# dP as rows of four heads in an attention backward pass, and V five heads ahead

## The chip, the cores and the metric

The kernel runs on one core of a Trainium2 chip. A core has five engines that run side by side: TensorE (PE, matmuls; PEld is its weight load), VectorE (DVE), ScalarE (ACT), GpSimd (POOL) and SyncE (SP, which only issues DMAs). They share an on-chip memory of 128 partitions (SBUF); TensorE writes into PSUM, eight banks of 512 fp32 columns in each partition. Sixteen DMA engines carry data between SBUF and the main memory; a 1 MB transfer is cut into sixteen parts, one for each of them, and has landed when the last part has. SP, ACT and POOL each issue transfers in the order of their own program. The metric is the time of one execution on the device, in microseconds (us).

## The reference

The reference is one decode step of a transformer block and its backward pass. Only the attention part matters here. There are 4 batches and 32 heads, so 128 pairs, called heads below (s = 0 to 127); each has a cache K and V of 4096 rows of 128 bf16 numbers, 1 MB each, and a single query row.

```python
scores = einsum("bhqd,bhkd->bhqk", q, k_cache) * Dh ** -0.5
p = softmax(scores)                                    # one row of 4096 per head
o = einsum("bhqk,bhkd->bhqd", p, v_cache)
h = x + o.reshape(...) @ wo                            # then a gated MLP
out, vjp = jax.vjp(f, x, k_cache, v_cache, wq, wo, w1, w3, w2)
grads = vjp(grad_out)
```

The outputs include the gradients of both caches. For one head, with dO the gradient of its output row, they are

- dV = p (a column of 4096) times dO (a row of 128),
- dP = V dO (4096 numbers), c = the sum of dO times o,
- dS = p (dP - c) scale, and dK = dS (a column) times q (a row).

So each head reads K and V in the forward pass, reads V again in the backward pass, and writes dV and dK: 3 MB a head in the backward pass.

## The kernel before

In the forward pass K and V stream through. The backward pass is one loop over the heads. SBUF holds 23 slots of 1 MB that are given out and given back in order; of these up to seven hold V for the loop, the others take dV and dK (`gv`, `gk`) and, early on, things of the forward pass. Position (p, j) of a head is row 32 p + j of its cache, p the partition, j from 0 to 31.

V has to be turned before dP can be computed, since TensorE sums over partitions: 32 transposes a head, in four groups of eight, each group copied back over V by ACT.

```python
def V_T(s, ps, part=range(SJ // GW)):                  # SJ = 32, GW = 8
    ...
    for g in part:
        pt = ps.tile([P, GW, P], BF16, tag="tps", name="pt_tps")
        for i in range(GW):
            nc.tensor.transpose(pt[:, i, :], v[:, g * GW + i, :], ident_b[:])
        nc.scalar.copy(out=v[:, g * GW:(g + 1) * GW, :], in_=pt[:])
```

`front(s)` turns V and computes dP with the turned V as the stationary operand: 32 weight loads of 128x128, each followed by a matmul with the one column of dO. `grad_K(s)` makes dS on VectorE, and dK by an outer product there; `grad_V(s)` makes dV in the same way from P and dO. Rows of dO and q are replicated over the partitions for four heads at a time (`reps`, two buffers of each).

```python
def outer(dst, col2, row):                             # VectorE, 128x4096 outputs
    nc.vector.tensor_tensor(out=dst..., in0=col2..., in1=row..., op=ALU.mult)

def grad_V(s):
    gv = Slot("gv")
    outer(gv.heads(), P2s.pop(s), reps["rdo", s // REP][:, s % REP, :])
    nc.gpsimd.dma_start(out=rows_of(out_3[b, h]), in_=gv.heads())
    ...

def front(s):
    if s % REP == 0:
        replicate(s)
    if s not in VTs:
        V_T(s, psT)
    VT = VTs[s].heads()
    dP_ps = psD.tile([P, SJ], FP32, name="dP_ps", tag="dP")
    for j in range(SJ):
        nc.tensor.matmul(dP_ps[:, j:j + 1], lhsT=VT[:, j, :], rhs=dOT_bf[:, s:s + 1], start=True, stop=True)
    sl = VTs.pop(s)
    (vring if len(V2s) + len(VTs) + len(vring) < NV2 else free).append(sl.i)   # NV2 = 7
    P_pairs(s + 2)                                     # GpSimd: P of a head, each number twice
    bwd[s] = dP_ps

def grad_K(s):
    dP_ps = bwd.pop(s)
    t = bw3.tile([P, SJ], FP32, tag="dSt", name="dSt")
    nc.vector.tensor_scalar(out=t[:], in0=dP_ps[:], scalar1=c_rep[:, s:s + 1], scalar2=scale, ...)
    dS2 = bw3.tile([P, SJ, 2], BF16, tag="dS2", name="dS2")
    nc.vector.tensor_tensor(out=dS2[:], in0=t..., in1=P_all[:, s]..., op=ALU.mult)
    gk = Slot("gk")
    outer(gk.heads(), dS2, reps["rq", s // REP][:, s % REP, :])
    nc.sync.dma_start(out=rows_of(out_2[b, h]), in_=gk.heads())
    gk.give()
```

The loop runs V one head ahead of dK, and dV one head ahead. ACT issues the loads of V (`prefetch`, `load_V2`). dV of heads 0 and 1 is made before the loop.

```python
front(0)
for s in range(NH):
    prefetch()
    if s + 1 < NH:
        ...                                            # load V of s + 1 if it has no slot yet
        front(s + 1)
        if s > 0:
            grad_V(s + 1)
    grad_K(s)
    if s >= S0:                                        # S0 = 21
        step("s", 1 if s < S0 + 38 else 3)             # side work, see below
    elif s >= O0:                                      # O0 = 2
        step("o")
```

The steps are side work woven in between the heads. First come the rest of dO with the turned pages of wo ("o"). Then come 128 small fp32 matmuls for dq, four pages of wq to be read, turned and multiplied, and the gradients of the weights ("s").

Of the kernel before, what the change touches and what calls it, by code (L numbers as in the profile page):

```python
# [9 lines left out]
FP32 = mybir.dt.float32  # L10
BF16 = mybir.dt.bfloat16
ALU = mybir.AluOpType
# [3 lines left out]
G = 2  # L16
# [8 lines left out]
def kernel(  # L25
# [22 lines left out]
    nc = tc.nc  # L48
    P = nc.NUM_PARTITIONS

    B = A_x.shape[0]
    D = A_x.shape[-1]
    H = A_k_cache.shape[1]
# [3 lines left out]
    NH = B * H  # L57
# [4 lines left out]
    SJ = Sk // P  # L62
    FC = F // P
    GW = 8
# [3 lines left out]
    scale = float(Dh) ** -0.5  # L68
# [28 lines left out]
    const = ctx.enter_context(tc.tile_pool(name="const", bufs=1))  # L97
    pers = ctx.enter_context(tc.tile_pool(name="pers", bufs=1))
    small = ctx.enter_context(tc.tile_pool(name="small", bufs=2))
    slotp = ctx.enter_context(tc.tile_pool(name="slotp", bufs=1))  # L100


    free = deque(range(NSLOT))

    class Slot:
# [52 lines left out]
    ident_f = const.tile([P, P], FP32, name="ident_f")  # L158
# [2 lines left out]
    nc.vector.tensor_copy(out=ident_b[:], in_=ident_f[:])  # L161
    ones_f = const.tile([P, P], FP32, name="ones_f")
    nc.gpsimd.memset(ones_f[:], 1.0)
    sel_f = const.tile([P, H], FP32, name="sel_f")
    nc.vector.tensor_copy(out=sel_f[:], in_=ident_f[:, 0:H])
    for q in range(1, P // H):
        nc.vector.tensor_tensor(out=sel_f[:], in0=sel_f[:], in1=ident_f[:, q * H:(q + 1) * H], op=ALU.add)
    onesw = []
    for i in range(2):
        t = const.tile([P, 64], BF16, name=f"onesw{i}")  # L170
        nc.gpsimd.memset(t[:], 0.0)
        nc.gpsimd.memset(t[:, 32 - i:33 - i], 1.0)
        onesw.append(t)

    def ones_window(col):
# [2 lines left out]

    rowg = const.tile([P, 8], FP32, name="rowg")
    nc.vector.tensor_reduce(out=rowg[:], in_=ident_f.rearrange("p (c g q) -> p g c q", c=4, q=4), axis=AX.XY, op=ALU.add)
    quad = const.tile([P, 4], FP32, name="quad")
    nc.vector.tensor_reduce(out=quad[:], in_=ident_f.rearrange("p (q i) -> p q i", q=4), axis=AX.X, op=ALU.add)
    bsum = const.tile([P, P], FP32, name="bsum")
    nc.vector.tensor_copy(out=bsum.rearrange("p (c g q) -> p c g q", c=4, q=4),
                          in_=rowg[:, None, :, None].to_broadcast([P, 4, 8, 4]))
    maskneg = const.tile([P, G], FP32, name="maskneg")
    nc.vector.tensor_scalar(out=maskneg[:], in0=rowg[:, 0:G], scalar1=-1.0, scalar2=1e30, op0=ALU.add, op1=ALU.mult)
    wmask = const.tile([P, G, 32], BF16, name="wmask")  # L190
    nc.gpsimd.memset(wmask[:], 0.0)
    for g in range(G):
        nc.vector.tensor_copy(out=wmask[:, g, 4 * g:4 * g + 4], in_=quad[:])
    selg = const.tile([G, P], FP32, name="selg")

    rstd_x = pers.tile([B, 1], FP32, name="rstd_x")
    xhatT = pers.tile([P, DC, B], BF16, name="xhatT")
    qT_bf = pers.tile([P, NH], BF16, name="qT_bf")
    qrep = pers.tile([P, 4, NH], BF16, name="qrep")
# [4 lines left out]
    P_all = pers.tile([P, NH, SJ], BF16, name="P_all")  # L204
# [53 lines left out]
    with ExitStack() as c0:  # L258
# [38 lines left out]
    psT = c1b.enter_context(tc.tile_pool(name="psT", bufs=2, space=bass.MemoryType.PSUM))  # L297
# [5 lines left out]
    def zq_window(z, m):  # L303
        a = 66 * (m % 2) + 32 + (m % 2) - m
        return z[:, a:a + 32]
# [371 lines left out]
    psT = c1b.enter_context(tc.tile_pool(name="psTm", bufs=4, space=bass.MemoryType.PSUM))  # L677
# [26 lines left out]
    assert not pending  # L704
    c1b.close()
    c1.close()


    pers2 = ctx.enter_context(tc.tile_pool(name="pers2", bufs=1, reuse_waits="tile"))
    O_sb = pers2.tile([NH, Dh], BF16, name="O_sb")  # L710
    dOT_bf = pers2.tile([P, NH], BF16, name="dOT_bf")
# [36 lines left out]
    REP = B  # L748
# [16 lines left out]
    def outer(dst, col2, row):  # L765
        nc.vector.tensor_tensor(  # L766
            out=dst.rearrange("p j (r t) -> p j r t", t=2),
            in0=col2[:, :, None, :].to_broadcast([P, SJ, Dh // 2, 2]),
            in1=row.rearrange("p (r t) -> p r t", t=2)[:, None, :, :].to_broadcast([P, SJ, Dh // 2, 2]),
            op=ALU.mult,  # L770
        )

    def grad_V(s):
        b, h = bh_of(s)
# [3 lines that stand above are left out]
        if s > 1:  # L778
            gv.give()
        else:  # L780
            first_gv.append(gv)
# [140 lines left out]

    with ExitStack() as c2:
        psT = c2.enter_context(tc.tile_pool(name="psT2", bufs=2, space=bass.MemoryType.PSUM))
        psD = c2.enter_context(tc.tile_pool(name="psD", bufs=2, space=bass.MemoryType.PSUM))
        psrep = c2.enter_context(tc.tile_pool(name="psrep", bufs=1, space=bass.MemoryType.PSUM))
        psg = c2.enter_context(tc.tile_pool(name="psg", bufs=2, space=bass.MemoryType.PSUM))
        psx = c2.enter_context(tc.tile_pool(name="psx", bufs=1, space=bass.MemoryType.PSUM))
# [202 lines left out]

        bwd = {}


        def P_pairs(s):
            if s < NH and s not in P2s:
                P2s[s] = bw3.tile([P, SJ, 2], BF16, tag="P2", name="P2")
                nc.gpsimd.tensor_copy(out=P2s[s][:], in_=P_all[:, s, :, None].to_broadcast([P, SJ, 2]))  # L1138

        def front(s):  # L1140
            if s % REP == 0:
                replicate(s)
            if s not in VTs:
                V_T(s, psT)
            VT = VTs[s].heads()
            dP_ps = psD.tile([P, SJ], FP32, name="dP_ps", tag="dP")
            for j in range(SJ):
                nc.tensor.matmul(dP_ps[:, j:j + 1], lhsT=VT[:, j, :], rhs=dOT_bf[:, s:s + 1], start=True, stop=True)  # L1148
            sl = VTs.pop(s)
            (vring if len(V2s) + len(VTs) + len(vring) < NV2 else free).append(sl.i)  # L1150
            P_pairs(s + 2)
            bwd[s] = dP_ps

        def grad_K(s):
            b, h = bh_of(s)
            dP_ps = bwd.pop(s)
            t = bw3.tile([P, SJ], FP32, tag="dSt", name="dSt")
            nc.vector.tensor_scalar(out=t[:], in0=dP_ps[:], scalar1=c_rep[:, s:s + 1], scalar2=scale,  # L1158
                                    op0=ALU.subtract, op1=ALU.mult)
            dS2 = bw3.tile([P, SJ, 2], BF16, tag="dS2", name="dS2")  # L1160
            nc.vector.tensor_tensor(out=dS2[:], in0=t[:, :, None].to_broadcast([P, SJ, 2]),  # L1161
                                    in1=P_all[:, s, :, None].to_broadcast([P, SJ, 2]), op=ALU.mult)
            gk = Slot("gk")
            outer(gk.heads(), dS2, reps["rq", s // REP][:, s % REP, :])
            nc.sync.dma_start(out=rows_of(out_2[b, h]), in_=gk.heads())
            gk.give()

        def prefetch():
            while nv["next"] < NH and vring:
                load_V2(nc.scalar)  # L1170


        O0, S0 = 2, 21
        front(0)
        for s in range(NH):
            prefetch()
            if s + 1 < NH:
                if s + 1 not in V2s and s + 1 not in VTs:
                    load_V2(nc.scalar)
                if s == 0:  # L1180

                    first_gv[0].give()
                front(s + 1)
                if s > 0:
                    grad_V(s + 1)
            grad_K(s)
            if s == 0:
                first_gv[1].give()
            if s >= S0:
                step("s", 1 if s < S0 + 38 else 3)  # L1190
            elif s >= O0:
                step("o")
# [31 lines left out]
```

## Time and profile before

| | |
|---|---|
| time, median of 3 runs | 1721.15 us (1721.13 to 1724.16) |
| span in the profile | 1720.0 us |
| moved by the DMAs | 707.86 MB, mean 412 GB/s |
| busy: PE, DVE, ACT, POOL | 1331.8, 1253.1, 960.3, 414.4 us |
| forward pass, backward pass | up to about 690 us, from about 705 us |

The profile page gives the busy time of each engine, then the span in 40 slices (43 us each) with the busy share in tenths, the TensorE clock that was granted, and the DMA rate; then the chain of work that ended last, and groups of instructions by line. A group's line ends with its busy time, the mean of one instruction in ns, and the idle time of the engine just before it with what released it. Views by stage give the same for any stretch of the span. In the timeline, every line is one instruction or a run of like ones: start, duration, engine, line of the kernel, operation, output and input.

### The profile page before, as it was taken

To read this page: it belongs to the slowest core of one execution; us is meant where nothing else is said; L and a number is where in the kernel's file an instruction comes from. 1 tells how busy PE (TensorE), PEld (TensorE's weight loads), DVE (VectorE), ACT (ScalarE), POOL (GpSimd) and SP (SyncE) were. 2 spreads that over 40 slices of the span, in tenths; PEclk is the share of its full clock that TensorE was granted. 3 is DMA by queue.
4 is the path that set the end of the run, shared out by engine and by line. 5 is a ranking of instruction groups with operands and counts; after the bars stand their busy time and mean duration, and the time that the engine had idled before them with its cause. 6 is when DMAs were issued, how large, how long until landed. Compare 5 with 4: busy or idle time off the path is not lost. (4 is left out here: it accounts for less than half of the span.)

```text
span 1720.0 us, 44172 instructions
## 1 busy us (share of the span) xinstructions
PE 1331.8 (77%) x19124; PEld 1131.8 (66%) x19124; DVE 1253.1 (73%) x1389; ACT 960.3 (56%) x1470; POOL 414.4 (24%) x689
## 2 busy tenths in 40 slices
PE   5889888888888888888788787883677778677852
PEld 4767766766667666877677777773565566555652
DVE  5989899899998997667676776763567557456575
ACT  3455444444454444677655555553676667676752
POOL 1211222222222231231322222321223122212220
PEclk8999999999999999666655555555875565565556
DMA  9999999999999999999999999999999999999996
GB/s 397 418 419 419 419 418 420 418 419 418 412 418 405 418 402 395 380 424 424 424 424 425 424 425 425 424 425 398 411 388 410 422 421 417 404 420 419 419 421 273
DMA packets 101762, 707.86 MB, mean 412 GB/s; under 512 B 11052, under 2 KB 15288, under 8 KB 17600
## 3 DMA queue, kind: packets, MB, share of 16 engines
q1 hardware_dynamic: 63568, 432.04, 60.9%
q0 software_dynamic: 20864, 148.22, 20.6%
q10 hardware_dynamic: 17136, 124.79, 17.7%
q8 instruction: 150, 2.46, 0.5%
q14 instruction: 44, 0.36, 0.1%
HBM read 422.59 MB, written 282.34 MB: 410 GB/s over the span
## 5 line engine op out<-in xcount | busy, mean ns | idle before, releaser
L761 ACT COPY V<-pt_tps 128x1024 bf16<-128x1024 bf16 x512 | 492.5, 1016 | 200.4 <-PE pt_tps L760 175.2
L760 PE MATMUL pt_tps<-ident_b,V 128*128 128x128 bf16 x4096 | 454.1, 293 | 82.9 <-ACT V L761 78.6
L760 PEld LDWEIGHTS <-V 128*128 128x128 bf16 x4096 | 402.7, 138 | 146.2 <-issue 137.1
L766 DVE TENSOR_TENSOR gv<-P,reps 128x4096 bf16<-128x4096 bf16 x125 | 287.2, 2297 | 195.8 <-ACT reps L1129 92.4
L766 DVE TENSOR_TENSOR gk<-dS,reps 128x4096 bf16<-128x4096 bf16 x128 | 294.0, 2297 | 113.5 <-DMA out_dram<-gv 90.8
L433 PE MATMUL M_ps<-PK,Vn 128*128 128x130 bf16 x4096 | 287.4, 223 | 46.4 <-DMA Vn<-in_A_v_cache_dram 44.3
L418 DVE TENSOR_TENSOR PK<-Kn,PK 128x4096 bf16<-128x4096 bf16 x128 | 292.3, 2284 | 31.7 <-POOL PK L414 31.4
L433 PEld LDWEIGHTS <-Vn 128*128 128x128 bf16 x4096 | 254.9, 100 | 67.1 <-DMA Vn<-in_A_v_cache_dram 59.2
L325 DVE STREAM_TRANSPOSE KT<-Kn 128x512 f32<-128x512 f32 (+1 forms) x321 | 250.6, 797 | 0.3 <-issue 0.2
L320 ACT COPY KT<-pt_tps 128x1024 bf16<-128x1024 bf16 x128 | 129.5, 1012 | 192.9 <-PE pt_tps L319 145.7
L777 POOL DMA_DIRECT2D out_dram<-gv x128 | 68.4, 534 | 673.2 <-DVE dSt L1158 581.9
L1148 PE MATMUL dP_ps<-dOT_bf,V 128*128 128x1 bf16 x4096 | 149.9, 166 | 83.4 <-ACT V L761 58.7
L1148 PEld LDWEIGHTS <-V 128*128 128x128 bf16 x4096 | 140.1, 103 | 96.8 <-ACT V L761 70.2
L1138 POOL COPY P<-P_all 128x64 bf16<-128x64 bf16 x125 | 157.8, 1263 | 0.0
L331 POOL TENSOR_TENSOR W<-qrep,wmask 128x128 bf16<-128x128 bf16 x128 | 123.6, 966 | 82.7 <-PE S_ps L351 67.8
L414 POOL COPY PK<-P_all 128x64 bf16<-128x64 bf16 x128 | 32.6, 255 | 421.4 <-ACT P_all L408 418.4
L408 ACT COPY P_all<-pt_P 32x64 bf16<-32x64 bf16 x256 | 52.1, 203 | 58.9 <-PE pt_P L404 56.7
L1129 ACT CAST reps<-rep_ps 128x512 bf16<-128x512 f32 x62 | 36.4, 587 | 83.8 <-PE rep_ps L1126 46.5
L319 PE MATMUL pt_tps<-ident_b,Kn 128*128 128x128 bf16 x1024 | 81.2, 224 | 0.0
L319 PEld LDWEIGHTS <-Kn 128*128 128x128 bf16 x1024 | 62.6, 100 | 25.8 <-issue 25.8
L443 PE MATMUL kP_ps<-PK,onesw 128*32 128x512 bf16 x1024 | 79.4, 387 | 0.0
L351 PE MATMUL S_ps<-KT,W 128*32 128x256 bf16 x1536 | 75.2, 285 | 0.5 <-DVE KT L325 0.2
(239 smaller groups left out, 1284.9 us busy)
## 6 DMA issues: line engine op xcount, KB each, us to landing
Kn<-in_A_k_cache_dram SPq DMA_DIRECT2D x128, 1024.0 KB, 15.7
Vn<-in_A_v_cache_dram SPq DMA_DIRECT2D x128, 1024.0 KB, 16.1
out_dram<-gv POOLq DMA_DIRECT2D x128, 1024.0 KB, 29.0
out_dram<-gk SPq DMA_DIRECT2D x128, 1024.0 KB, 22.7
V<-in_A_v_cache_dram ACTq DMA_DIRECT2D x119, 1024.0 KB, 15.1
V<-in_A_v_cache_dram SPq DMA_DIRECT2D x9, 1024.0 KB, 18.7
wq<-in_A_wq_dram SPq DMA_DIRECT2D x8, 1024.0 KB, 19.0
out_dram<-gw POOLq DMA_DIRECT2D x6, 896.0 KB, 38.3
```

The source lines that it names most:

```text
L319: nc.tensor.transpose(pt[:, i, :], Kn[:, c * GW + i, :], ident_b[:])
L320: nc.scalar.copy(out=KT[:, c * GW:(c + 1) * GW, :], in_=pt[:])
L325: nc.vector.transpose(out=KT[:, c * w_:(c + n) * w_], in_=Kn[:, c * w_:(c + n) * w_])
L331: nc.gpsimd.tensor_tensor(out=W[:, hl], in0=qrep[:, :, s:s + 1].to_broadcast([P, 4, 32]), in1=wmask[:, hl, None, :].to_broadcast([P, 4, 32 ...
L418: nc.vector.tensor_tensor(out=PK[:, :, 0:Dh].rearrange("p j (r t) -> p j r t", t=2), in0=Ks[s].heads().rearrange("p j (r t) -> p j r t", t=2),
L433: nc.tensor.matmul(hold["M"][:], lhsT=Vn[:, j, :], rhs=PK[:, j, :], start=(j == 0), stop=(j == SJ - 1))
L443: nc.tensor.matmul(hold["kP"][32 * q:32 * (q + 1), :, :], lhsT=ones_window(w), rhs=PK[:, j0:j0 + 4, 0:Dh], start=(w == 0 and c == 0), stop ...
L760: nc.tensor.transpose(pt[:, i, :], v[:, g * GW + i, :], ident_b[:])
L761: nc.scalar.copy(out=v[:, g * GW:(g + 1) * GW, :], in_=pt[:])
L766: nc.vector.tensor_tensor(out=dst.rearrange("p j (r t) -> p j r t", t=2), in0=col2[:, :, None, :].to_broadcast([P, SJ, Dh // 2, 2]), in1=r ...
L1138: nc.gpsimd.tensor_copy(out=P2s[s][:], in_=P_all[:, s, :, None].to_broadcast([P, SJ, 2]))
L1148: nc.tensor.matmul(dP_ps[:, j:j + 1], lhsT=VT[:, j, :], rhs=dOT_bf[:, s:s + 1], start=True, stop=True)
```

## The change

dO becomes the stationary operand and the turned V the moving one. A stationary operand of 32 columns, all zero but for one that holds dO, lets a matmul put its result into one row of 32 and add zero to the others; `zq_window(z, m)` is the slice of a zeroed tile that has dO in column m. Four such matmuls sit in the four column groups of the array (`tile_position`). In this way four heads, with two rows for each quarter of their positions, fill rows of one PSUM bank. ACT copies the bank out, four fp32 transposes turn it, and VectorE makes dS of four heads at once. So dK of a group of four can only begin when V of all four heads is through. The loop therefore runs V five heads ahead of dK, and dV three, and replicates rows four heads ahead. It is meant to take 32 weight loads a head away from TensorE and to let VectorE work on when TensorE is held up. Constants of the forward pass move to a pool (`fcon`) that is closed before the backward pass, which makes room.

```diff
-        psD = c2.enter_context(tc.tile_pool(name="psD", bufs=2, space=bass.MemoryType.PSUM))
+        psD = c2.enter_context(tc.tile_pool(name="psD", bufs=1, space=bass.MemoryType.PSUM))
...
+        zd = [bw3.tile([P, 132], BF16, name=f"zd{i}", tag=f"zd{i}", bufs=1) for i in range(B)]
+        for i in range(B):
+            nc.gpsimd.memset(zd[i][:], 0.0)
+        def dO_window(s):
+            nc.gpsimd.tensor_copy(out=zd[s % B][:, 32:132:67], in_=dOT_bf[:, s:s + 1].to_broadcast([P, 2]))
...
+        def rows_out():
+            if "ps" in rows:
+                rows["sb"] = bw3.tile([P, 512], FP32, tag="dPr", name="dPr", bufs=1)
+                nc.scalar.copy(out=rows["sb"][:], in_=rows.pop("ps")[:])
+        def rows_T():
+            if "sb" in rows:
+                sb = rows["t"] = rows.pop("sb")
+                rows["T"] = psD.tile([P, B, P], FP32, tag="dPT", name="dPT_ps")
+                for jj in range(4):
+                    nc.tensor.transpose(rows["T"][:, jj, :], sb[:, jj * P:(jj + 1) * P], ident_f[:])
         def front(s):
-            if s % REP == 0:
-                replicate(s)
+            hl = s % B
             if s not in VTs:
-                V_T(s, psT)
+                for g in range(SJ // GW):
+                    V_T(s, psT, range(g, g + 1))
+                    if hl == 0 and g == 0:
+                        rows_out()
+                    if hl == 0 and g == 2:
+                        rows_T()
             VT = VTs[s].heads()
-            dP_ps = psD.tile([P, SJ], FP32, name="dP_ps", tag="dP")
-            for j in range(SJ):
-                nc.tensor.matmul(dP_ps[:, j:j + 1], lhsT=VT[:, j, :], rhs=dOT_bf[:, s:s + 1], start=True, stop=True)
+            if hl == 0:
+                rows["acc"] = psD.tile([P, 512], FP32, tag="dP", name="dP_ps")
+            dO_window(s)
+            for u in range(2):
+                for c in range(4):
+                    j0 = 8 * c + 4 * u
+                    nc.tensor.matmul(rows["acc"][32 * c:32 * (c + 1), :], lhsT=zq_window(zd[hl], 2 * hl + u),
+                                     rhs=VT[:, j0:j0 + 4, :], start=(hl == 0 and u == 0),
+                                     stop=(hl == B - 1 and u == 1), tile_position=(0, 32 * c))
...
+        def group_dS(g):
+            ...
+            for hl in range(B):
+                nc.vector.tensor_scalar(out=t5[:, hl], in0=T[:, :, 2 * hl:2 * hl + 2, :], scalar1=c_rep[...], scalar2=scale, ...)
+            dS2s[g] = bw3.tile([P, B, SJ, 2], BF16, tag="dS2", name="dS2", bufs=1)
+            nc.vector.tensor_tensor(out=dS2s[g][:], in0=t..., in1=P_all[:, i0:i0 + B]..., op=ALU.mult)
...
-        O0, S0 = 2, 21
-        front(0)
+        O0, S0, L, LV = 2, 21, 5, 3
+        for s in range(L):
+            load_ahead(s)
+            P_pairs(s)
+            front(s)
+            if s < 2:
+                first_gv[s].give()
+            elif s < LV + 1:
+                grad_V(s)
+        group_dS(0)
         for s in range(NH):
...
+            load_ahead(s + L)
+            if s % REP == 0 and s + REP < NH:
+                replicate(s + REP)
+            P_pairs(s + L)
+            if s + L < NH:
+                front(s + L)
+            elif s + L == NH:
+                rows_out()
+                rows_T()
+            if s > 0 and s + LV < NH:
+                grad_V(s + LV)
             grad_K(s)
-            if s == 0:
-                first_gv[1].give()
+            if s % B == B - 1 and s + 1 < NH:
+                group_dS((s + 1) // B)
```

More of the change, by code (lines that the diff above doesn't have):

```diff
@@ L100 @@
     slotp = ctx.enter_context(tc.tile_pool(name="slotp", bufs=1))
+    cF = ExitStack()
+    fcon = cF.enter_context(tc.tile_pool(name="fcon", bufs=1))
     free = deque(range(NSLOT))
@@ L163 @@
     nc.gpsimd.memset(ones_f[:], 1.0)
-    sel_f = const.tile([P, H], FP32, name="sel_f")
+    sel_f = fcon.tile([P, H], FP32, name="sel_f")
     nc.vector.tensor_copy(out=sel_f[:], in_=ident_f[:, 0:H])
@@ L169 @@
     for i in range(2):
-        t = const.tile([P, 64], BF16, name=f"onesw{i}")
+        t = fcon.tile([P, 64], BF16, name=f"onesw{i}")
         nc.gpsimd.memset(t[:], 0.0)
@@ L177, in ones_window @@
         return onesw[i][:, 32 - i - col:64 - i - col]
-    rowg = const.tile([P, 8], FP32, name="rowg")
+    rowg = fcon.tile([P, 8], FP32, name="rowg")
     nc.vector.tensor_reduce(out=rowg[:], in_=ident_f.rearrange("p (c g q) -> p g c q", c=4, q=4), axis=AX.XY, op=ALU.add)
-    quad = const.tile([P, 4], FP32, name="quad")
+    quad = fcon.tile([P, 4], FP32, name="quad")
     nc.vector.tensor_reduce(out=quad[:], in_=ident_f.rearrange("p (q i) -> p q i", q=4), axis=AX.X, op=ALU.add)
-    bsum = const.tile([P, P], FP32, name="bsum")
+    bsum = fcon.tile([P, P], FP32, name="bsum")
     nc.vector.tensor_copy(out=bsum.rearrange("p (c g q) -> p c g q", c=4, q=4),
                           in_=rowg[:, None, :, None].to_broadcast([P, 4, 8, 4]))
-    maskneg = const.tile([P, G], FP32, name="maskneg")
+    maskneg = fcon.tile([P, G], FP32, name="maskneg")
     nc.vector.tensor_scalar(out=maskneg[:], in0=rowg[:, 0:G], scalar1=-1.0, scalar2=1e30, op0=ALU.add, op1=ALU.mult)
-    wmask = const.tile([P, G, 32], BF16, name="wmask")
+    wmask = fcon.tile([P, G, 32], BF16, name="wmask")
     nc.gpsimd.memset(wmask[:], 0.0)
@@ L193 @@
         nc.vector.tensor_copy(out=wmask[:, g, 4 * g:4 * g + 4], in_=quad[:])
-    selg = const.tile([G, P], FP32, name="selg")
+    selg = fcon.tile([G, P], FP32, name="selg")
     rstd_x = pers.tile([B, 1], FP32, name="rstd_x")
@@ L198 @@
     qT_bf = pers.tile([P, NH], BF16, name="qT_bf")
-    qrep = pers.tile([P, 4, NH], BF16, name="qrep")
+    qrep = fcon.tile([P, 4, NH], BF16, name="qrep")
     d_hhT = pers.tile([P, FC, B], FP32, name="d_hhT")
@@ L706 @@
     c1.close()
+    cF.close()
     pers2 = ctx.enter_context(tc.tile_pool(name="pers2", bufs=1, reuse_waits="tile"))
@@ L1130, in replicate @@
                 reps[nm_, i0 // REP] = rt
-        bwd = {}
+        rows = {}
+        dS2s = {}
+        zd = [bw3.tile([P, 132], BF16, name=f"zd{i}", tag=f"zd{i}", bufs=1) for i in range(B)]
[3 more added lines that the diff above has]
+            nc.gpsimd.tensor_copy(out=zd[s % B][:, 32:132:67], in_=dOT_bf[:, s:s + 1].to_broadcast([P, 2]))
         def P_pairs(s):
@@ L1149, in front @@
+            if hl == B - 1:
+                rows["ps"] = rows.pop("acc")
             sl = VTs.pop(s)
             (vring if len(V2s) + len(VTs) + len(vring) < NV2 else free).append(sl.i)
-            P_pairs(s + 2)
-            bwd[s] = dP_ps
+        def group_dS(g):
+            i0 = g * B
+            T = rows.pop("T").rearrange("p jj (c m) -> p c m jj", c=4)
+            t = rows.pop("t")[:, 0:B * SJ].rearrange("p (b j) -> p b j", b=B)
+            t5 = t.rearrange("p b (c u jj) -> p b c u jj", c=4, u=2)
+            for hl in range(B):
+                nc.vector.tensor_scalar(out=t5[:, hl], in0=T[:, :, 2 * hl:2 * hl + 2, :], scalar1=c_rep[:, i0 + hl:i0 + hl + 1],
+                                        scalar2=scale, op0=ALU.subtract, op1=ALU.mult)
+            dS2s[g] = bw3.tile([P, B, SJ, 2], BF16, tag="dS2", name="dS2", bufs=1)
+            nc.vector.tensor_tensor(out=dS2s[g][:], in0=t[:, :, :, None].to_broadcast([P, B, SJ, 2]),
+                                    in1=P_all[:, i0:i0 + B, :, None].to_broadcast([P, B, SJ, 2]), op=ALU.mult)
@@ L1154, in grad_K @@
         def grad_K(s):
             b, h = bh_of(s)
[L1156 to L1162, printed above, removed]
@@ L1163, in grad_K @@
             gk = Slot("gk")
-            outer(gk.heads(), dS2, reps["rq", s // REP][:, s % REP, :])
+            outer(gk.heads(), dS2s[s // B][:, s % B], reps["rq", s // REP][:, s % REP, :])
             nc.sync.dma_start(out=rows_of(out_2[b, h]), in_=gk.heads())
@@ L1170, in prefetch, with load_ahead @@
                 load_V2(nc.scalar)
-        O0, S0 = 2, 21
-        front(0)
-        for s in range(NH):
[L1176 to L1179, printed above, removed]
-                if s == 0:
[L1182 to L1185, printed above, removed]
+        O0, S0, L, LV = 2, 21, 5, 3
+        def load_ahead(s):
+            prefetch()
+            if s < NH and s not in V2s and s not in VTs:
+                load_V2(nc.scalar)
+        for s in range(L):
[7 more added lines that the diff above has]
+        group_dS(0)
+        for s in range(NH):
+            load_ahead(s + L)
[9 more added lines that the diff above has]
+                grad_V(s + LV)
             grad_K(s)
-            if s == 0:
-                first_gv[1].give()
+            if s % B == B - 1 and s + 1 < NH:
+                group_dS((s + 1) // B)
             if s >= S0:
```

## The prediction

> **What bounds the kernel now.** I read the page's 40 slices first, then the busy time by stage, then how DMAs land, then the timeline at the start of the backward pass.
>
> The slices show a kernel that lives on its DMAs:
>
> ```profile
> PEclk8999999999999999666655555555875565565556
> DMA  9999999999999999999999999999999999999996
> GB/s 397 418 419 419 419 418 420 418 419 418 412 418 405 418 402 395 380 424 424 424 424 425 424 425 425 424 425 398 411 388 410 422 421 417 404 420 419 419 421 273
> ```
>
> DMA is full in every slice but the last, at 418 to 425 GB/s; no compute engine is. Clear dips are in slices 13 to 17 (down to 380), 28 to 31 (down to 388) and the last. By stage of the backward pass (start, end, busy us of each engine, clock, DMA share, GB/s):
>
> ```profile
> 688.00:731.00 43.00, 37.66 (x662) 35.20 (x660) 26.63 (x43) 28.81 (x35) 9.80 (x13) 0.68 0.96 380
> 731.00:860.00 129.00, 102.93 (x1475) 92.95 (x1473) 89.26 (x82) 91.62 (x103) 36.20 (x39) 0.65 1.01 424
> 860.00:1161.00 301.00, 246.16 (x2921) 230.95 (x2919) 207.80 (x171) 167.20 (x183) 81.35 (x86) 0.52 1.01 425
> 1161.00:1290.00 129.00, 75.64 (x1150) 68.44 (x1147) 66.93 (x59) 70.34 (x79) 24.51 (x28) 0.72 0.98 399
> 1290.00:1634.00 344.00, 261.35 (x2969) 203.54 (x2967) 204.41 (x173) 237.27 (x308) 77.34 (x105) 0.58 1.01 417
> ...
> 1700.00:1704.00 4.00, 0.00 (x0) 0.00 (x0) 0.00 (x0) 0.00 (x0) 0.00 (x0) 0.50 0.98 410
> 1704.00:1720.00 16.00, 0.00 (x0) 0.00 (x0) 0.00 (x0) 0.00 (x0) 0.00 (x0) 0.50 0.08 32
> ```
>
> The last row is the key. All compute ended at 1699.6 us; after 1704 the DMA share is 0.08, and after 1708 it is 0.06, one sixteenth: one of the 16 DMA engines works alone for 15 us, at full speed (8 KB in 306 ns). I then took from the trace when each sixteenth of each 1 MB transfer landed. The last sixteenth trails the eighth by 1.5 us at 50 us, 6 us at 500 us and 13 us at 1165 us. From 722 us to the end there are always at least five transfers issued whose last sixteenth has not landed. So one slow engine has work without a break from 722 us on, and it ends the program. The dips at 1161 to 1290 us are the other fifteen engines running dry while the slow one catches up: they cost nothing. The one place where it starves is the start of the backward pass, about 705 to 722 us, with only two or three transfers under way.
>
> ```profile
> 708.58 2.28 DVE L766 TENSOR_TENSOR gv<-reps 128x4096 bf16<-128x4096 bf16 x1
> ...
> 711.67 2.29 DVE L766 TENSOR_TENSOR gk<-dS,reps 128x4096 bf16<-128x4096 bf16 x1
> 715.20 2.29 DVE L766 TENSOR_TENSOR gv<-reps 128x4096 bf16<-128x4096 bf16 x1 [1.23 <-DMA out_dram<-gv]
> ...
> 718.00 2.29 DVE L766 TENSOR_TENSOR gk<-dS,reps 128x4096 bf16<-128x4096 bf16 x1
> 720.21 2.32 DVE L766 TENSOR_TENSOR gv<-P,reps 128x4096 bf16<-128x4096 bf16 x1
> ```
>
> The reader should see that dV and dK come out in turn, the first dK already at 711.67 us. Each such 1 MB is 2.5 us of DMA.
>
> **What the skill says.** Four places bear on this. "DMA: Bandwidth & Descriptors", section "Latency and other measured facts", says that engines 7 and 15 are usually slower in traces and guesses at the descriptor rings of GpSimd's DMAs. This trace agrees with one slow engine, and its lag grows faster once dV is written from the GpSimd queue (from 2 to 13 us between 750 and 1165 us, against 0.6 to 6 us in the first 500); which engine it is, the records do not show. "Runtime: NRT & Kernel Launch", section "Instruction fetch mechanics", says instructions come in 16 KiB blocks through a DMA queue; the page has it as q8, 150 packets, 2.46 MB. "TensorE: Matmul & The Clock Gate", Part 3, says that four matmuls of 32 columns each run side by side; the trace agrees: eight 32x512 matmuls of the forward pass (kP) took 0.62 us together, while one alone lasts 0.39. Its Part 1 says the array runs at half clock unless it was busy through a whole window of 3.4 us; the trace agrees with a clock of 0.50 to 0.72 in the backward pass.
>
> **The change, part by part.** The groups it touches:
>
> ```profile
> L1148 PE MATMUL dP_ps<-dOT_bf,V 128*128 128x1 bf16 x4096 | 149.9, 166 | 83.4 <-ACT V L761 58.7
> L1148 PEld LDWEIGHTS <-V 128*128 128x128 bf16 x4096 | 140.1, 103 | 96.8 <-ACT V L761 70.2
> L443 PE MATMUL kP_ps<-PK,onesw 128*32 128x512 bf16 x1024 | 79.4, 387 | 0.0
> ```
>
> - *TensorE.* Removed: 4096 one-column matmuls, 149.9 us of busy time, 1.17 us a head. Added: 8 matmuls of 512 columns a head. At full clock they should cost what kP costs, 0.62 us; at half clock two rounds of 0.43 us (512 columns at 1.2 GHz, an estimate from Part 1 of that page) and 0.2, about 1.05 us. Added too: four fp32 transposes per four heads, by estimate 0.5 us each (six fp32 passes of dq take 1.42 us, and a transpose is two passes), so 0.5 us a head. Busy time therefore stays about equal: 150 us off, about 80 to 135 plus 64 on. What matters is which part waits for ACT. Before, 24 of the 32 dP matmuls ran under ACT's last copy, and 8 (0.35 us) after it. Now the fourth and the last four wait for that copy: about 0.9 us at half clock. A head's chain (ACT copies 3.9 us, gaps, dP, next transposes) gets longer by about 0.55 us, plus 0.15 for ACT's 0.59 us copy of the rows and 0.45 for the transposes.
> - *VectorE.* Per head 0.24 + 0.23 us go; per four heads four 0.25 us operations and one of about 0.5 us come: 0.1 us a head saved, and it waits on DMA anyway.
> - *GpSimd.* One small copy more per head (0.2 us alone, up to 2 us when VectorE is in its way, as the P copy shows: 0.25 to 2.07 us). It stands in front of dP, so TensorE now waits for GpSimd's order of work.
> - *Instruction fetch.* 6112 fewer TensorE instructions in the order of instructions; 2.46 MB over 38,248 records of TensorE makes 64 bytes each, so 0.39 MB, 24 of the 150 blocks. Each block took 0.88 to 0.97 us; spread over 16 engines, about 1.4 us for the slow engine; over eight, 2.8. I take -2 us.
> - *The start.* Now five fronts (transposes and dP of heads 0 to 4) come before the first dK, with only two dV writes between. Front 0 waits for GpSimd's new memsets and window, so head 1's transposes start near 714 us instead of 711. A front took ACT 5.2 us a head; with the longer dP, 6. Fronts 1 to 3 end near 732, the third part of front 4, the row transposes and dS near 739: the first dK is computed at about 739 to 742 us instead of 711.67. From 716 to 742 us the DMA has dV of heads 2 and 3 and two loads of V: 4 MB, 10 us of work in 26. That is 16 us idle, where now there are 3 to 4 (380 GB/s and 0.96 share in that stage). With the slow engine's lag: **+11 us**.
> - *Steady state.* The DMA pace is 7.6 us a head (3 MB). The chain of TensorE and ACT before, at half clock in the dq stretch, is 6.65 us plus 0.4 for the replicated rows; after, 6.65 + 0.55 + 0.15 + 0.45 + 0.4 = 8.2 us at half clock, and by the same steps about 6.8 at full clock. A TensorE that is the bound is also busy through whole windows, so the clock should rise often enough. I charge **+2 us** for stretches where it does not.
>
> Sum: 1721 - 2 + 11 + 2 = **1732 us**.
>
> **The rivals.** (a) *The lead pays.* V five heads and dV three heads ahead of dK let VectorE write on while TensorE is stuck, as in the waits of 16.5 us (dSt on dP) and 15.5 us (dV on the replicated rows) near 1190 and 1245 us. For it: those stages fall to 399 GB/s. Against: the slow engine kept five or more transfers in hand all through. If I read that wrongly, up to 8 us come back there, about 1713 to 1720. (b) *The chain becomes the bound.* At 8.2 us a head for the 43 heads of the dq stretch, 0.6 x 43 = 26 us would be lost: about 1755. For it: the clock stood at 0.50 for over 200 us there, with TensorE 82% busy. Against: the removed one-column matmuls are replaced by wide ones, and DMA needs only 7.6. (c) *The start costs nothing*, because the loads queued before it last longer than I think: then 1721. Against: only two transfers were in flight at 711 us.
>
> **Range and chances.** The lower end is (c) with the fetch gain and part of (a): 1716. The upper end is half of (b) on top of my sum, and a little: 1750. For 2% faster, 1687, the slow engine would have to lose 34 us of work, and the bytes are the same: 1%. For 2% slower, above 1755.6, (b) must hold nearly in full: 7%. Within 2%: 92%.
>
> **What would show it.** Right: DMA still 9 in nearly all slices; a hole of some 10 us more between 712 and 745, with the first dK near 740; the last compute followed by the same lone-engine tail; q8 near 126 packets; dP busy time of 80 to 135 us; VectorE's waits near 1190 and 1245 shorter, without a gain from it. Wrong: no hole at the start; GB/s under 415 in 860 to 1161 with ACT or TensorE as the releaser of VectorE's idle time (then the chain is the bound); a tail without the lone engine (then the order of transfers matters, and the slow engine is not the floor).

## The result and the profile after

| | before | after |
|---|---|---|
| time, median | 1721.66 us (1721.13 to 1724.16, 4 runs) | 1715.18 us (1713.99 to 1716.50, 4 runs) |
| ratio | | 0.996, 95% interval 0.9942 to 0.9977 |
| span in the profile | 1720.0 us | 1714.6 us |
| moved by the DMAs | 707.86 MB | 707.49 MB |

The changed kernel is 6.5 us faster. I had predicted 1732 us, with a lower end of 1716; the time lies just under that end.

The 40 slices of the changed kernel, the granted TensorE clock in tenths, DMA share in tenths and GB/s:

```profile
PEclk9999999999999999998888886876878786677886
DMA  9999999999999999799999999999999999999998
GB/s 400 424 424 424 425 423 424 424 423 422 420 423 411 419 408 399 296 407 425 424 424 423 424 423 424 423 425 424 390 383 372 425 425 421 422 423 423 424 424 337
```

Three things stand out against the slices of before. The hole at the start of the backward pass is there as foretold: slice 17 has 296 GB/s instead of 380. But slices 2 to 10, in the forward pass, which the change of dP does not touch, run at 422 to 425 GB/s instead of 418 to 420. And the TensorE clock in the backward pass is mostly 0.6 to 0.8, where it was mostly 0.5 or 0.6.

By stage (start, end, busy us of PE, PEld, DVE, ACT and POOL, clock, DMA share, GB/s), with the same cuts as in the prediction:

```profile
688.00:731.00 43.00, 31.72 (x458) 24.22 (x458) 20.67 (x35) 28.21 (x34) 5.90 (x26) 0.90 0.73 287
731.00:860.00 129.00, 90.18 (x1016) 60.85 (x1015) 84.42 (x64) 90.39 (x104) 36.19 (x56) 0.89 1.01 422
860.00:1161.00 301.00, 217.31 (x2012) 155.50 (x2010) 200.08 (x141) 172.94 (x199) 83.73 (x127) 0.80 1.01 424
1161.00:1290.00 129.00, 74.78 (x797) 54.70 (x795) 66.45 (x46) 68.69 (x78) 43.06 (x46) 0.77 0.98 399
1290.00:1634.00 344.00, 252.48 (x2070) 158.89 (x2067) 200.44 (x147) 243.66 (x323) 112.66 (x147) 0.75 1.00 417
...
1704.00:1715.00 11.00, 0.00 (x0) 0.00 (x0) 0.00 (x0) 0.00 (x0) 0.00 (x0) 0.50 0.16 67
```

The first row fell from 380 to 287 GB/s: that is the hole. The others are what they were (422 to 424, then 399, then 417): DMA is the bound of the steady state in both kernels, and the new dP does not disturb it. In the last row the DMA share is 0.16, well over one sixteenth: the last engine is no longer alone all that time. In the records of landings, the last sixteenth trails the fifteenth by 1.6 us at the end, where it trailed by 11.4 us before.

The timeline of VectorE at the start of the backward pass (start, duration, line, operation; in brackets the idle time ahead and what ended it):

```profile
706.58 2.29 DVE L770 TENSOR_TENSOR gv<-reps 128x4096 bf16<-128x4096 bf16 x1 [3.16 <-PE dP_ps L1178]
709.98 2.29 DVE L770 TENSOR_TENSOR gv<-P,reps 128x4096 bf16<-128x4096 bf16 x1 [1.10 <-POOL P L1148]
724.78 0.73 DVE L1192 TENSOR_SCALAR dPr<-dPT_ps,c_rep 128x32 f32<-128x32 f32 x4 [12.51 <-PE dPT_ps L1160]
725.54 0.42 DVE L1195 TENSOR_TENSOR dS<-dPr,P_all 128x256 bf16<-128x256 f32 x1
726.00 2.29 DVE L770 TENSOR_TENSOR gk<-dS,reps 128x4096 bf16<-128x4096 bf16 x1
```

The first dK starts at 726.00 us instead of 711.67. VectorE stands idle for 12.51 us ahead of its dS, waiting for TensorE's turned rows. In that time the trace has only one or two transfers under way. The groups of the new dP:

```profile
L1178 PE MATMUL dP_ps<-V,zd 128*32 128x512 bf16 x1024 | 180.4, 453 | 83.7 <-ACT V L765 61.7
...
L1178 PEld LDWEIGHTS <-zd 128*32 128x32 bf16 x1024 | 36.5, 96 | 169.9 <-issue 136.3
```

The count is 1024 instead of 4096, and the weight loads fell from 140 us to 36.5. The queue of instruction blocks (packets, MB, share of 16 engines) has 127 packets instead of 150:

```profile
q8 instruction: 127, 2.08, 0.5%
```

So the hole is there, the order is as foretold, and yet the kernel is faster: something worth more than the hole had no place in my sum.

### The profile page after: what moved, and what is told of

Same layout as the page of the kernel before. It is cut to its first block, busy times and chain, and to the rows that moved or that the text cites. A ratio compares the mean times of both kernels' runs of the same rounds, so it can differ in the third digit from the quotient of the medians.

```text
span 1714.6 us, 38302 instructions
## 1 busy us (share of the span) xinstructions
PE 1271.0 (74%) x16180; PEld 944.0 (55%) x16180; DVE 1228.3 (72%) x1293; ACT 969.3 (57%) x1502; POOL 472.3 (28%) x823
## 2 busy tenths in 40 slices
DMA packets 101740, 707.49 MB, mean 413 GB/s; under 512 B 11052, under 2 KB 15288, under 8 KB 17600
## 5 line engine op out<-in xcount | busy, mean ns | idle before, releaser
L765 ACT COPY V<-pt_tps 128x1024 bf16<-128x1024 bf16 x512 | 491.4, 1024 | 194.9 <-PE pt_tps L764 126.8
L764 PE MATMUL pt_tps<-ident_b,V 128*128 128x128 bf16 x4096 | 370.7, 254 | 144.5 <-ACT V L765 138.9
L764 PEld LDWEIGHTS <-V 128*128 128x128 bf16 x4096 | 320.1, 117 | 214.5 <-issue 206.0
L421 DVE TENSOR_TENSOR PK<-Kn,PK 128x4096 bf16<-128x4096 bf16 x128 | 292.3, 2283 | 26.3 <-POOL PK L417 25.8
L1178 PE MATMUL dP_ps<-V,zd 128*32 128x512 bf16 x1024 | 180.4, 453 | 83.7 <-ACT V L765 61.7
L1148 POOL COPY P<-P_all 128x64 bf16<-128x64 bf16 x127 | 134.1, 1056 | 0.0
L1178 PEld LDWEIGHTS <-zd 128*32 128x32 bf16 x1024 | 36.5, 96 | 169.9 <-issue 136.3
L1192 DVE TENSOR_SCALAR dPr<-dPT_ps,c_rep 128x32 f32<-128x32 f32 x128 | 23.1, 242 | 128.4 <-PE dPT_ps L1160 128.2
L1143 POOL COPY zd<-dOT_bf 128x2 bf16<-128x2 bf16 x128 | 93.3, 729 | 3.0 <-PE dP_ps L1178 3.0
```

What stands on the lines that cost most here:

```text
L421: nc.vector.tensor_tensor(out=PK[:, :, 0:Dh].rearrange("p j (r t) -> p j r t", t=2), in0=Ks[s].heads().rearrange("p j (r t) -> p j r t", t=2),
L1143: nc.gpsimd.tensor_copy(out=zd[s % B][:, 32:132:67], in_=dOT_bf[:, s:s + 1].to_broadcast([P, 2]))
L1178: nc.tensor.matmul(rows["acc"][32 * c:32 * (c + 1), :], lhsT=zq_window(zd[hl], 2 * hl + u), rhs=VT[:, j0:j0 + 4, :], start=(hl == 0 and u ...
```

## The experiments

Each set of runs (e1 to e4, e5 to e8, e9 and e10, e11) had the kernel before beside it on the same chip. The sets lie on three chips, but its median was 1722.1 to 1722.4 us in all of them, so times of different sets are compared below. My first theory came from the slices: the forward pass moves more bytes a second, and the only part of the change that can act there is the move of the constants. It shifts the base of the 23 slots. From the allocation of the built programs: each slot takes 8320 bytes of a partition, 65 x 128, so all slots share one offset within 128 bytes. Before, the first one starts at byte 32992, which is 32 past a multiple of 64 and 96 past one of 128; after, at 30336, a multiple of 128. The rival was that the new dP and the longer lead had brought the gain.

### Where the slots start

**e1: the kernel before, with 32 unused bytes ahead of the slots.**

```diff
+    padp = ctx.enter_context(tc.tile_pool(name="padp", bufs=1))
+    pad_t = padp.tile([P, 16], BF16, name="pad_t")
+    nc.gpsimd.memset(pad_t[:], 0.0)
     slotp = ctx.enter_context(tc.tile_pool(name="slotp", bufs=1))
```

> The kernel before with 32 unused bytes per partition ahead of the 23 slots: the slots then start on a multiple of 64 bytes (33024), as in the changed kernel, instead of 32 past one (32992). Nothing else differs. Theory A (the gain is where the DMAs land: slots on 64-byte bounds): the forward pass goes from 418 to 424 GB/s and ends about 8 us earlier, no hole at 705 to 735 us appears, and the time is 1709 to 1714 us. Theory B (the forward pass was faster for another reason, such as the program's own shape or the placement of its tensors in main memory): 1720 to 1723 us.

Measured: 1713.54 us (1712.63 to 1716.99), ratio 0.9954 (0.9942 to 0.9967). Thirty-two unused bytes are worth as much as the whole change.

**e3: the same with 64 bytes** (a tile of 32 columns), so that the slots keep their old offset within 64 bytes.

> The kernel before with 64 unused bytes: the slots move, but stay 32 bytes past a multiple of 64. Theory A: as before, 1720 to 1723 us, forward pass at 418 GB/s. If any move of the slots helps (theory B'), it is as fast as with 32 bytes.

Measured: 1721.47 us (1719.95 to 1724.41), ratio 0.9998 (0.999 to 1.0006). So it isn't the unused tile, nor its memset, but the offset.

**e2: the changed kernel with 32 unused bytes** ahead of the slots, which takes its alignment away.

> The changed kernel with the same 32 bytes, which push its slots off the 64-byte bounds. Theory A: the forward pass falls back to 418 GB/s, the hole at the start of the backward pass stays, and the time is 1723 to 1730 us, slower than the kernel before. Theory B: no change, 1714 to 1717 us.

Measured: 1721.25 us (1719.55 to 1724.79), ratio 0.9997 (0.9989 to 1.0006). I had expected it slower than the kernel before; it is level with it. Without the alignment, all the rest of the change together is worth nothing that can be told from zero.

**e4: the kernel before, with the constants moved and nothing else.**

```diff
+    cF = ExitStack()
+    fcon = cF.enter_context(tc.tile_pool(name="fcon", bufs=1))
...
-    sel_f = const.tile([P, H], FP32, name="sel_f")
+    sel_f = fcon.tile([P, H], FP32, name="sel_f")
... (the other constants and qrep likewise; cF.close() ahead of the backward pass)
```

> The kernel before with one part of the change alone: the constants of the forward pass go to the pool that is closed early, and dP stays as it was. The slots start at 30336, a multiple of 64, as in the changed kernel. Theory A: as fast as with 32 bytes of padding, 1709 to 1714 us. Theory B (what was gained comes from the new dP and its lead): 1720 to 1723 us.

Measured: 1714.36 us (1712.89 to 1716.31), ratio 0.9954 (0.9941 to 0.9968). This part alone brings the gain. The median is 0.4 us above the range I gave.

**e8: the kernel before, with 96 unused bytes** (a tile of 48 columns): slots at a multiple of 64 bytes, but 64 past one of 128.

> The kernel before with 96 unused bytes ahead of the slots: they start at 64 mod 128 bytes (before: 32 mod 64; with 32 unused bytes: 0 mod 128). If 64 bytes are the grain: 8 KB packets of the forward pass at 312 ns and 1712 to 1716, as with 32 bytes. If 128 are needed: 316 ns and 1720 to 1723.

Measured: 1722.44 us (1720.34 to 1724.02), ratio 0.9999 (0.9991 to 1.0007). I had thought 64 bytes would do; they don't. Offsets of 32, 64 and 96 past a multiple of 128 are equally slow in these runs, and 0 is fast.

The stage 60 to 640 us, the body of the forward pass, in the kernel before:

```profile
60.00:640.00 580.00, 491.44 (x8177) 404.64 (x8177) 529.34 (x702) 289.19 (x641) 147.93 (x342) 0.99 1.01 416
```

in e8 (64 past a multiple of 128):

```profile
60.00:640.00 580.00, 492.01 (x8170) 404.37 (x8168) 529.08 (x701) 289.18 (x641) 147.58 (x342) 0.99 1.01 416
```

and in e4 (a multiple of 128):

```profile
60.00:640.00 580.00, 495.64 (x8273) 407.51 (x8270) 534.89 (x709) 290.93 (x647) 150.69 (x348) 0.99 1.01 421
```

The last figure is GB/s. DMA is full in all three (share 1.01); in e4 the same full engines move 1.2% more. The packet records show where: in this stage an 8 KB packet of the loads of K and V takes 316.6 ns on average in the kernel before, 316.4 in e8, and 312.4 in e4, where nine packets in ten take 309. By 663 us e4 is some 8 us ahead of the kernel before in its landings. In the backward pass (800 to 1150 us) the packets of both take 310 to 312 ns, and there the alignment gains nothing further. Why an offset slows a packet, the records do not show.

### The hole, the order and the instructions

The rest of the change came out near zero: 1714.36 us with only the constants moved, 1715.18 with everything. But the landings show the hole. Transfers are counted here in the order in which their last sixteenth lands. The slowest sixteenth of the 289th transfer lands at 730.4 us in e4 and at 737.0 in the changed kernel, 6.6 us later. The changed kernel is still 7.8 us behind at the 457th (1158.9 and 1166.7) and 6.9 at the 550th; at the end it is level (1712.0 and 1712.2). Something in the backward pass gives the loss back. Two candidates: the order (V and dV further ahead), or the 6000 fewer TensorE instructions, which must be fetched by the same DMA engines.

**e6: constants moved, the new order, but the old dP.** Each dP is still 32 one-column matmuls, and ACT copies it out, a copy a head that e4 does not have.

```diff
+        def dP_out(s):
+            if s in dPs:
+                bwd[s] = bw3.tile([P, SJ], FP32, name="dP_sb", tag="dPsb", bufs=6)
+                nc.scalar.copy(out=bwd[s][:], in_=dPs.pop(s)[:])
...
-        front(0)
-        for s in range(NH): ... front(s + 1) ... grad_V(s + 1) ... grad_K(s)
+        for s in range(L): load_ahead(s); P_pairs(s); front(s); ...        # L, LV = 5, 3
+        for s in range(NH): ... front(s + L) ... grad_V(s + LV) ... grad_K(s)
```

> The kernel before with the constants moved (aligned slots) and the new order (V five heads, dV three heads ahead of dK), but dP still as 32 one-column matmuls a head, copied out by ACT. The instruction count stays that of before. Theory lead (the order gives back what the hole cost): the last sixteenth loses about 8 us at the start and gains it back by the end as in the changed kernel, total 1713 to 1716, slow engine's lag at the end 1 to 4 us. Theory fetch (the 6000 fewer TensorE instructions give it back): no give-back, total 1720 to 1724, lag 9 to 12 us. Theory of the chain (TensorE and ACT too slow with old dP and more copies): over 1724 with GB/s under 415 in 860 to 1161 us.

Measured: 1719.96 us (1717.55 to 1722.38, 21 runs), ratio 0.9986 (0.9979 to 0.9992). The order, with these copies, costs 5.6 us against e4 in the medians, and nothing is given back. The time is at the lower end of what the fetch theory expected. The lag is not: at the end the last sixteenth trails the fifteenth by 5.3 us, between the two expectations. Its timeline has an idle stretch at the start too, with another releaser:

```profile
724.16 2.29 DVE L770 TENSOR_TENSOR gv<-P,reps 128x4096 bf16<-128x4096 bf16 x1 [11.59 <-ACT reps L1133]
```

Here dV of head 4 waits 11.59 us for the replicated rows, which stand behind five heads' copies in ACT's order. So a long lead fills the start of the loop with ACT work whichever form dP has. But only a part of the loss arises there. By the landings, e6 is 1.9 us behind e4 at the 300th transfer, 1.5 at the 457th, 7.1 at the 550th and 2.6 at the end (the two profiled executions lie closer together than the medians). The rates show two places, first in e4, then in e6:

```profile
690.00:740.00 50.00, 42.15 (x671) 38.74 (x670) 35.39 (x42) 35.13 (x41) 16.11 (x19) 0.67 0.95 370
1161.00:1290.00 129.00, 79.15 (x1185) 70.85 (x1184) 73.33 (x67) 74.33 (x84) 28.96 (x30) 0.74 0.99 399
690.00:740.00 50.00, 40.06 (x691) 36.26 (x688) 29.84 (x33) 35.18 (x47) 15.32 (x21) 0.74 0.91 350
1161.00:1290.00 129.00, 78.67 (x1069) 72.35 (x1067) 66.64 (x55) 66.58 (x85) 31.71 (x30) 0.63 0.94 388
```

**e5: the changed kernel with the hole filled.** dV needs no dP. So dV of heads 4 and 5 is made ahead of the first dK, and dV stays five heads ahead; the rows of dO are replicated earlier.

```diff
-        O0, S0, L, LV = 2, 21, 5, 3
+        O0, S0, L, LV = 2, 21, 5, 5
...
             front(s)
+            if s == 1:
+                replicate(REP, ("rdo",))
...
+        P_pairs(L)
+        grad_V(L)
         group_dS(0)
...
-                replicate(s + REP)
+                replicate(s + REP, ("rq",))
+            if s % REP == 2 and s + REP + 2 < NH:
+                replicate(s + REP + 2, ("rdo",))
```

> The changed kernel with dV five heads ahead instead of three (dV of heads 4 and 5 are written before the first dK; the replicated rows of dO come one group earlier). Slots stay 64-byte aligned. Theory A (the hole at the start costs and is given back only in part): 2 MB more, 5 us of work, go into the hole of 702 to 730 us; the GB/s of 690 to 740 us rises from 300 to 340 or more, and the end comes 2 to 6 us earlier, 1709 to 1713. Theory B (the hole is given back in full later, the end is set by the slow engine's own later work): hole filled, end unchanged, 1714 to 1716.

Measured: 1708.33 us (1707.87 to 1710.63), ratio 0.9922 (0.9909 to 0.9934): faster than both kernels, and 6.9 us faster than the changed one (the intervals of the two ratios do not overlap). Its timeline:

```profile
714.51 2.29 DVE L770 TENSOR_TENSOR gv<-P,reps 128x4096 bf16<-128x4096 bf16 x1 [1.11 <-POOL P L1148]
717.91 2.29 DVE L770 TENSOR_TENSOR gv<-P,reps 128x4096 bf16<-128x4096 bf16 x1 [1.11 <-POOL P L1148]
726.51 0.73 DVE L1192 TENSOR_SCALAR dPr<-dPT_ps,c_rep 128x32 f32<-128x32 f32 x4 [6.31 <-PE dPT_ps L1160]
727.27 0.42 DVE L1195 TENSOR_TENSOR dS<-dPr,P_all 128x256 bf16<-128x256 f32 x1
727.73 2.29 DVE L770 TENSOR_TENSOR gk<-dS,reps 128x4096 bf16<-128x4096 bf16 x1
```

The first two lines are dV of heads 4 and 5; the wait ahead of the first dS fell from 12.51 to 6.31 us, though dS itself is no earlier. The slowest sixteenth of the 289th transfer lands at 730.8 us instead of 737.0, and in the profiled runs the gain of 6.2 us there is 4.6 us at the end. The hole did cost, then, and wasn't made good for free by what comes later. The rate from 690 to 740 us rose from 300 to 330 GB/s, less than the 340 I expected; the time came out just under the 1709 to 1713 us of theory A.

**e10: dV seven heads ahead**, with heads 6 and 7 in the hole as well.

```diff
-        O0, S0, L, LV = 2, 21, 5, 5
+        O0, S0, L, LV = 2, 21, 5, 7
...
-        P_pairs(L)
-        grad_V(L)
+        for s in range(L, LV + 1):
+            P_pairs(s)
+            grad_V(s)
```

> The filled kernel with dV seven heads ahead instead of five: dV of heads 6 and 7 are also written before the first dK. If the rest of the hole (VectorE's 6.3 us ahead of the first dS, 330 GB/s in 690 to 740 us) still costs and slots are free: GB/s in 690 to 740 us over 355 and the end at 1703 to 1707. If slots or GpSimd's copies of P stand in the way, or the loads of V are pushed back instead: 1707 to 1711.

Measured: 1709.86 us (1709.11 to 1715.34), ratio 0.9924 (0.991 to 0.9937): no better than e5. VectorE no longer waits ahead of the first dS, and 690 to 740 us moves 348 GB/s, under the 355 I expected. The profiled execution was the slowest of the five (1715.34 us), so its landings don't tell why the rest of the hole is worth nothing; this stays open.

**e9: e5 with the instruction count of before.** Ninety-six one-column matmuls, whose results are overwritten, ahead of each group of four dPs.

```diff
                 rows["acc"] = psD.tile([P, 512], FP32, tag="dP", name="dP_ps")
+                for _ in range(96):
+                    nc.tensor.matmul(rows["acc"][0:32, 0:1], lhsT=VT[:, 0, 0:32], rhs=dOT_bf[:, s:s + 1],
+                                     start=True, stop=True)
```

> The filled kernel (1708.3 us) plus 96 one-column matmuls with a 32-column weight load ahead of each group of four dPs, whose results are overwritten: 6144 TensorE instructions more, so that the count is that of before (37,628 against 37,500) and the instruction blocks rise from 127 to about 151. Theory fetch (the blocks take DMA time from the engine that ends last): from 730 us to the end the last sixteenth takes 4 to 9 us longer, total 1712 to 1717. Rival (the shorter backward pass of the changed kernel comes from the order of work or from its chain, and not from the fetch): 1707 to 1710, with 151 blocks all the same. A third (the added 0.9 us of TensorE work a head makes the chain the bound): over 1717, GB/s under 415 in 860 to 1161 us.

Measured: 1717.90 us (1715.34 to 1720.00), ratio 0.9972 (0.9961 to 0.9983): 9.6 us slower than e5, and 0.9 above the range of the fetch theory. The queue of instruction blocks:

```profile
q8 instruction: 151, 2.47, 0.5%
```

and the steady state:

```profile
860.00:1161.00 301.00, 246.16 (x3057) 188.46 (x3055) 200.17 (x141) 173.13 (x198) 72.36 (x126) 0.77 1.01 425
```

DMA is as full there as ever (425 GB/s), so the added work didn't make TensorE the bound in this stage. From the landing of the 289th transfer to the end the slowest sixteenth takes 985.0 us, against 976.8 in e5.

**e11: the control.** Eight wide matmuls in place of the 96: the group has 64.5 us of busy time (82.8 in e9), but 512 instructions in place of 6144.

```diff
-                for _ in range(96):
-                    nc.tensor.matmul(rows["acc"][0:32, 0:1], lhsT=VT[:, 0, 0:32], rhs=dOT_bf[:, s:s + 1], ...)
+                for _ in range(8):
+                    nc.tensor.matmul(rows["acc"][0:32, :], lhsT=VT[:, 0, 0:32], rhs=VT[:, 0:4, :], start=True, stop=True)
```

> The control for e9: the filled kernel plus 8 wide matmuls (512 columns) ahead of each group of four dPs, whose results are overwritten: as much or more added TensorE time as the 83 us of e9's one-column matmuls, but only 512 instructions instead of 6144, two instruction blocks instead of 24. If the blocks cost e9 its 9.6 us: 1707 to 1711 here. If the added time of TensorE did: 1715 to 1720.

Measured: 1710.62 us (1709.53 to 1712.27), ratio 0.9932 (0.9918 to 0.9945), inside the range expected if the blocks cost e9 its time.

```profile
q8 instruction: 129, 2.11, 0.5%
```

```profile
860.00:1161.00 301.00, 223.62 (x2142) 156.41 (x2140) 200.45 (x141) 174.78 (x202) 71.89 (x127) 0.85 1.01 425
```

The 22 blocks between e11 and e9 make 7.3 us, the 24 between e5 and e9 make 9.6: 0.33 to 0.40 us for each block of 16 KB. By the intervals of the ratios, each of these differences is uncertain by some 3 us, so 0.2 to 0.5 us a block is what the runs bear out.

The control isn't perfect. The added weight loads take 23.0 us in e11 and 79.8 in e9, and TensorE's total busy time rose less in e11, since its clock rose too (0.85 in this stage against 0.77 in e9). From 1161 to 1290 us e9 moves 393 GB/s, where e5 has 405 and e11 406. So a part of e9's loss may be TensorE's time.

The landings of all these kernels fit the blocks as well. From the landing of the 300th transfer, behind the hole, the last sixteenth needs 951.5 to 953.3 us to the end in all eight kernels with 150 or 151 blocks, whatever their order, form of dP or slots. It needs 941.4 to 946.4 us in four of the five with 127 to 129 blocks, and 949.4 in the slow execution of e10. TensorE's busy time goes the same way (1318 to 1337 us against 1251 to 1286), so the landings alone don't part the two. That the blocks carry most of it is the reading that fits the control and e6; how much is TensorE's own stays open.

### The slow DMA engine

**e7: constants moved, and dV written from SyncE's queue** instead of GpSimd's.

```diff
-        nc.gpsimd.dma_start(out=rows_of(out_3[b, h]), in_=gv.heads())
+        nc.sync.dma_start(out=rows_of(out_3[b, h]), in_=gv.heads())
```

> The kernel before with the constants moved (aligned slots), and dV written from SyncE's queue instead of GpSimd's. If the slow engine's growing lag in the backward pass (2 to 13 us between 750 and 1165 us) comes from GpSimd's queue: the lag stays under 6 us, the end comes 4 to 8 us earlier, 1706 to 1710. If the lag has another cause: 1713 to 1716 with the lag as before. If SyncE's order of dV and dK writes holds things up: slower, over 1718.

Measured: 1713.75 us (1712.11 to 1717.11), ratio 0.9953 (0.994 to 0.9965), the same as e4. The lag shrank: at the 457th transfer the last sixteenth trails the eighth by 5.0 us, where e4 has 11.3, e1 10.8 and the kernel before 12.6. (Behind the fifteenth it is 0.9 us against 9.2 in e4. But e1, with dV in GpSimd's queue, has only 2.6 there, since two sixteenths trail together in it; so the eighth is the safer mark.) But the stage from 860 to 1161 us moved less than e4's 425 GB/s:

```profile
860.00:1161.00 301.00, 230.93 (x2828) 216.45 (x2828) 194.79 (x161) 162.84 (x179) 10.68 (x42) 0.56 1.01 417
```

In return it has no dip after it (413 GB/s from 1161 to 1290 us, where e4 has 399). Over both stages e7 moves 415.8 GB/s and e4 417.2 (each rate weighted by its 301 or 129 us). So most of the lag goes with the GpSimd queue, as the prediction read it, but taking it away makes nothing faster. I had expected 4 to 8 us. What holds both to the same average stays open.

## Why the prediction was wrong

Step by step, with medians of the runs above:

| step | kernel | time |
|---|---|---|
| | before | 1722.2 us |
| constants moved (slots at a multiple of 128 bytes) | e4 | 1714.4, -7.8 |
| order: V five, dV three ahead (and a copy of dP by ACT) | e6 | 1720.0, +5.6 |
| dP as rows of four heads | the changed kernel | 1715.2, -4.8 |
| dV five ahead: hole filled | e5 | 1708.3, -6.9 |
| instruction count put back | e9 | 1717.9, +9.6 |

- **The step that failed first has no number in the prediction: the move of the constants.** I took it for what it says, a way to make room, and the sum has no term for it. It is worth -7.8 us (e4), more than the whole change. The alignment is the cause, as e1, e3 and e2 show: given to the kernel before by 32 unused bytes, withheld from it by 64, and taken from the changed kernel. With that one term, the sum of 1732 would have been 1724, still 9 us above the measured time.
- **"Instruction fetch ... I take -2 us" was mis-sized.** The count was right: 24 blocks fewer foretold, 23 measured. The cost of a block was not. I divided each block by 16 or 8 engines. Here a block costs the end 0.3 to 0.4 us by the medians, so 23 of them make some 7 to 9 us, an estimate from e9 and e11, with TensorE's own share not fully taken out. The step from e6 to the changed kernel, 4.8 us, points the same way, though the intervals of the two ratios only just part. The Trainium skill, "Runtime: NRT & Kernel Launch", section "Instruction fetch mechanics", calls the cost of crossing to a new block mostly hidden; that may hold for the engine that runs the instructions, but where DMA is the bound, these runs show it in the time.
- **"The start: +11 us" had the right mechanism and somewhat too large a size.** The hole is there (287 GB/s), with the first dK at 726 us and not at 739 to 742: a front took ACT 5.0 us and not 6, with TensorE's clock at 1.0 from 710 to 725 us. In landings the loss is 6.6 us at the 289th transfer and 7.8 at the 457th; e5, which fills half of the hole, gains 6.9. The whole change against e4 is +0.8 us; with the 7 to 9 us of the fetch taken off, the order and hole cost some 8 to 10 us by subtraction.
- **"Steady state: +2 us" was not needed.** From 860 to 1161 us the changed kernel moves 424 GB/s, before 425. The clock rose from 0.52 to 0.80 in this stage. dP's busy time, 180.4 us, is above the 80 to 135 I gave: 453 ns for each wide matmul; the fp32 transposes took 26.3 us and not 64. It costs nothing that shows in this stage: weight loads fell by 104 us, and DMA sets the pace. Rival (b), the chain as the bound, did not happen.
- **Rival (a), the lead pays, fell.** It named the right range, 1713 to 1720, for a wrong reason: the stage from 1161 to 1290 us stays at 399 GB/s, and in e6, which has the lead without the new dP, it falls to 388. VectorE is still held up there: its long waits of before (11.34, 16.54 and 15.49 us) became three of 14.85, 10.52 and 18.52 us on the turned rows.
- **Rival (c), the start costs nothing, fell** with slice 17.
- **The floor of the slow engine** held for reading where a loss counts. But the tail of one lone engine that I expected did not come: 1.6 us of lag and not 11.4. The prediction took that lag for the floor of the kernel's time; e7 shows that most of it goes with the queue, without the end moving. One reading was off, too: in the kernel before, the transfers under way from 722 us on are not "always at least five": at times they are only two to four, up to 778 us.

Roughly, then: a gain of 8 us that I had at nothing, some 6 us too little for the fetch and some 4 us too much for hole and chain make 18 us, against the 16.8 us by which the prediction was too high. Since the cost of the hole is taken by subtraction here, this adds up of itself; its own measure is the 6.6 to 7.8 us of the landings.

## What to carry to other kernels

When a change moves, adds or removes any on-chip tile, compare the addresses of the large buffers before and after: in this DMA-bound kernel an offset of 32 to 96 bytes was a term of its own, and a few unused bytes test it in one run. Compare the stages that the change should not touch first; a difference there names a cause that the diff's main part can't have. In a DMA-bound kernel, count the blocks of instructions that a change adds or takes away, since their fetch takes DMA time, and when work is put ahead in a loop, fill the start with whatever does not need the thing that is waited for.

## What the runs showed of the hardware

- Loads into on-chip slots that start 32, 64 or 96 bytes past a multiple of 128 took 316.3 to 316.6 ns per 8 KB packet in the forward pass (60 to 640 us), against 312.0 to 312.7 ns for slots at a multiple of 128: 416 against 421 GB/s, 8 us of 1722. In the backward pass, with reads and writes mixed, no difference was seen (310 to 312 ns in the kernel before and in e4). Whether a multiple of 256 would be better still wasn't tried; every other slot here is at an odd multiple of 128.
- A 16 KB block of instructions, some 1.0 us of one packet, goes with 0.33 to 0.40 us of this DMA-bound kernel's time by the medians (0.2 to 0.5 with their uncertainty). Which engines carry the blocks, the records do not show.
- With dV written from SyncE's queue instead of GpSimd's, the last sixteenth of the 457th transfer trails the eighth by 5.0 us instead of 11.3, at the same time in total (1713.75 and 1714.36 us).
